# A gated linear attention with a gated scan behind it: second group's attention ahead of the first projection, and an input weight that comes in two halves

## The chip, the cores and the metric

One core of one Trainium2 chip runs the whole kernel. The metric is the device time of one execution in microseconds (us). TensorE (PE) does matmuls and transposes, VectorE (DVE) scans and element-wise work, ScalarE (ACT) activations and copies, GpSimd (POOL) element-wise work, SyncE (SP) only hands out transfers. ACT and POOL can hand out transfers too.

## The reference

Two blocks, joined by a change of layout. All data are float32 but for the weights of the second block: these arrive as 64-bit floats (8 bytes an element), and the kernel makes 32-bit floats of them itself.

```python
# q, k, v, alpha: (B=4, H=8, S=768, D=48)
for t in range(S):
    state = alpha[:, :, t, :, None] * state + einsum('bhd,bhe->bhde', k[:, :, t], v[:, :, t])
    y[:, :, t] = einsum('bhd,bhde->bhe', q[:, :, t], state)
x = y.transpose(0, 2, 1, 3).reshape(B, S, 384)

proj = x @ w_in                      # w_in: (384, 1024)
val, gate = proj[..., :512], proj[..., 512:]
h = 0
for t in range(S):
    h = exp(A_log) * h + val[:, t]
    ys[:, t] = h
out = (silu(gate) * ys) @ w_out      # w_out: (512, 384)
```

## The kernel before, in words

The work is cut into N = 12 groups of GC = 256 positions, three for each batch entry, in order; a group has two chunks (c = 0, 1) of 128. Each group goes through two parts.

**Attention of a group.** Its alpha, k and q are loaded (`load_natural` L420 for the first three groups, `load_raw` L405 after these), v too (`load_v` L429). The first three groups are turned on PE (`natural_alpha` L556, `natural_qk` L567), the later ones on DVE (L590). `products` makes running products of alpha with a scan on DVE (prod, L599) and their inverses with a second (inv, L611). k times inv and q times prod make the tile Z (L573; `k_times`, `q_times`). Then `scores` (PE, L645), `keys` (PE transposes of Z, L635, copied by ACT to ktm, L636), `masks` (A: half by DVE from PSUM, L653, half copied by ACT, L651, and multiplied by POOL, L652), `values` (PE, L664), `state` (PE, L685, copied by ACT to S_sb, L688, for the next chunk; the next `state` adds to the same PSUM tile st, so it follows that copy), `carried` (PE, L675). `join` copies the result to xT (ACT, L694 and L695) and moves pieces of it between partitions with six small transfers (L698), handed out by POOL for groups 0 and 1, by SP and ACT for later ones.

**Projection of a group.** `project(n, cc)` for cc = 0 to 3 multiplies xT with columns cc of w_in (pv and pg, L713); `gated` scans pv on DVE (hh, L720), takes silu of pg on ACT (sg, L725) and multiplies both on POOL (f, L726). `output` multiplies f with w_out (L734), ACT copies (L738), SP stores (L739).

**Weights.** The bits of w_in lie over 128 partitions in bits_in: heads 0 to 3 (192 rows of w_in) on partitions 0 to 63, heads 4 to 7 on partitions 64 to 127. Four transfers bring them (L443): partitions 0-47, 64-111, 48-63, 112-127. The bits of w_out come in two (L448). `convert(i)` makes float32 of one quarter of the columns of w_in (i < NI = 4) or one half of w_out (i = 4, 5): ACT prepares wr from the low words (L510), DVE shifts and joins the high words (L511, L513), POOL adds both (L515). wr has two buffers. A float32 column quarter is needed by `project(n, cc)` of the same number.

**Order.** It is written out by hand: each engine takes its instructions in the order of the program text, and so do the queues of transfers of SP and ACT. Eight completion semaphores are shared by the transfers of SP and ACT in turn, so a transfer also waits for the one eight before it. The text has a prologue (loads of groups 0 and 1 and of the weights, attention of group 0, products of group 1, `warm`, which runs five matmuls that nobody reads), and then the loop over n = 0 to 11, in which iteration n projects group n, does attention of group n + 1, products of group n + 2, and loads group n + 3. Iterations 0 and 1 differ from the others: in iteration 0 the conversions stand between the projections, in iteration 1 Z of group 2 is made. The buffers of alpha, k and q are two per name (group modulo 2), those of v too; Z, hh, sg and the rest have two; PSUM has three tiles "mm" for pv, pg, output and transposes.

At the end a flag tells whether the running products stayed in range; a second, general function would run if not. It does not run with these inputs.

Of the kernel before, what the change touches and what calls it, by code (L numbers as in the profile page):

```python
# [346 lines left out]
def fast(  # L347
# [18 lines left out]
    nc = tc.nc  # L366
    B, H, S, D = q.shape
# [3 lines left out]
    G = 2  # L371
    GC = G * C
    NG = S // GC
    N = B * NG
    NT = GC // 32
    NK = DM // C
    NI = DI // C
    R = D - 32
# [47 lines left out]
    def load_v(m, engine, cs=range(G)):  # L426
        b, g = divmod(m, NG)
        for c in cs:
            engine.dma_start(out=vs[m % NV][:, c, :, 0:D],  # L429
                             in_=v[b, :, ds(g * GC + c * C, C), :].rearrange("h p d -> p h d"))  # L430
# [6 lines left out]
    bits_in = const.tile([C, NK, 2 * DI, 2], U32, name="bits_in")  # L437
    bits_out = const.tile([C, NI, DM, 2], U32, name="bits_out")

    def load_w_in(engine):  # L440

        for row, size, first, step in ((0, D, 0, D), (64, D, 4 * D, D), (D, R, 3 * D, R), (64 + D, R, 7 * D, R)):
            engine.dma_start(out=bits_in[ds(row, size)].rearrange("p kk n two -> p kk (n two)"),  # L443
                             in_=moe_w_in.bitcast(U32)[ds(first, NK * step)]
                             .rearrange("(kk p) n -> p kk n", p=step)[0:size])
# [51 lines left out]
    def convert(i):  # L497


        if i < NI:  # L500
            bits = bits_in.rearrange("p kk (vg n) two -> p kk vg n two", vg=2)[:, :, :, ds(i * C, C)]
            w = w_in[:, :, :, ds(i * C, C)]
        else:
            rows = ds(2 * (i - NI), 2)
            bits, w = bits_out[:, rows, None], w_out[:, rows, None, :]
        lo, hi = bits[..., 0], bits[..., 1]
        _, x, y, z = w.shape
        r = p2.tile([C, x, y, z], I32, tag="wr", name="wr")
        t = w.bitcast(U32)
        nc.scalar.activation(r, lo, AF.Copy, scale=2.0 ** -29)  # L510
        nc.vector.tensor_scalar(out=t, in0=hi, scalar1=3, scalar2=0x3FFFFFFF,  # L511
                                op0=ALU.logical_shift_left, op1=ALU.bitwise_and)
        nc.vector.scalar_tensor_tensor(out=t, in0=hi, scalar=0xC0000000, in1=t,  # L513
                                       op0=ALU.bitwise_and, op1=ALU.bitwise_or)
        return lambda: nc.gpsimd.tensor_tensor(out=w.bitcast(I32), in0=w.bitcast(I32), in1=r, op=ALU.add)  # L515
# [43 lines left out]
    def natural_qk(m, name):  # L559

        if m not in Zs:
            Zs[m] = p2.tile([C, 4, 2, GC], FP32, tag="Z", name="Z")
        tps = []
        for c in range(G):
            tp = ps_sc.tile([C, 4, C], FP32, tag=f"sc{c}", name="tn")
            for p in range(4):
                nc.tensor.transpose(tp[:, p, :], natural(name, m)[:, c, 2 * p:2 * p + 2, :], ident)  # L567
            tps.append(tp)

        def times(c):  # L570
            i, by = {"k": (1, invs), "q": (0, prods)}[name]
            cols = ds(c * C, C)
            nc.vector.tensor_mul(Zs[m][:, :, i, cols], tps[c], by[:, :, cols])  # L573
        return times
# [73 lines left out]
    def masks(m, c):  # L648
        A, sc = As[m, c]
        mb = mask[:, None, :].to_broadcast([C, 4, C])  # L650
        nc.scalar.activation(A[:, 1], sc[1], AF.Copy)  # L651
        nc.gpsimd.tensor_mul(A[:, 1], A[:, 1], mb)  # L652
        nc.vector.tensor_mul(A[:, 0], sc[0], mb)  # L653
# [94 lines left out]
    def pair(name, m, one, other):  # L748
        load_natural(name, m, 0, one)
        load_natural(name, m, 1, other)  # L750
# [5 lines left out]
    pair("q", 0, SP, SP)  # L756
    pair("a", 1, SP, SP)
    load_v(0, SP)
    load_w_in(SP)
    pair("k", 1, SP, SP)  # L760
    pair("q", 1, SP, SP)
    for i in range(2):
        load_w_out(i, SP)
    load_v(1, SP)

    constants()

# [9 lines left out]
    for name in "akq":  # L777
        pair(name, 2, SP, SP)

    def warm():  # L780

        t = ps_mm.tile([C, 4, C], FP32, tag="mm", name="warm")
        for _ in range(5):
            nc.tensor.matmul(t, ident, ident[:, None, :].to_broadcast([C, 4, C]), start=True, stop=True)

    warm()
    for _ in products(0):
        pass
    for c in range(G):
# [3 lines left out]
        scores(0, c)  # L793
    for c in range(G):
        masks(0, c)
    for c in range(G):
        keys(0, c)
    natural_alpha(1)
# [7 lines left out]
    state(0, 1)  # L806
    carried(0, 1)
    join(0, (nc.gpsimd, nc.gpsimd))
    convert(0)()
    warm()  # L810
    k_times, q_times = natural_qk(1, "k"), natural_qk(1, "q")
    for _ in steps:
        pass
    for c in range(G):
        k_times(c)
        q_times(c)

    checks = itertools.chain.from_iterable(check_w(i) for i in range(NW))
    value = None
    for n in range(N):  # L820
        m = n + 1
        att = m < N
        nat = n + 2 < NAT
        steps = products(n + 2) if n + 2 < N else iter(())

        def go(count):
            for _ in range(count):
                next(steps, None)


        if n + 3 < N:
            loads(n + 3)
        if n + 2 < N:
            load_v(n + 2, SP)

        def attend():
            for c in range(G):
                keys(m, c)
            for c in range(G):
                scores(m, c)  # L840


        pj = project(n, 0)
        gated(n, 0, *pj)
        if n == 0:
            convert(1)()
        if n == 1:
            for c in range(G):
                k_times(c)
                q_times(c)  # L850
        elif att:
            attend()
        if not nat:
            go(1)
        if n == 1:
            pj = project(n, 1)
            gated(n, 1, *pj)
            attend()
        if att:
            for c in range(G):  # L860
                masks(m, c)
        if n == 0:
            convert(2)()
        if n != 1:
            pj = project(n, 1)
            gated(n, 1, *pj)
        if n == 0:
            convert(3)()
        if not nat:
            go(1)  # L870
        pj = project(n, 2)
        gated(n, 2, *pj)
        if n == 0:
            convert(4)()
            convert(5)()
        if not nat:
            go(2)
        if att:
            state(m, 0)
            values(m, 0)  # L880
            values(m, 1)
            state(m, 1)
            carried(m, 0)
            carried(m, 1)
            join(m, (nc.gpsimd, nc.gpsimd) if n == 0 else (SP, ACT))
        pj = project(n, 3)
        gated(n, 3, *pj)
        if nat:
            natural_alpha(n + 2)
            check_alpha(n + 2)  # L890
        go(10)
        if 3 <= n:
            for _ in itertools.islice(checks, 2):
                pass
        if n == N - 2:
            check_end()
        if n == N - 1:
            value = nc.values_load(flag[0:1, 0:1], min_val=0, max_val=1)
        output(n)
        if nat:  # L900
            k_times, q_times = natural_qk(n + 2, "k"), natural_qk(n + 2, "q")
    return value


# [36 lines left out]
```

## Time and profile before

| | |
|---|---|
| median of 9 runs | 329.07 us (328.16 to 331.33) |
| the profiled execution, its own time | 326.13 us |
| its span in the profile | 324.3 us |
| PE busy | 292.2 us (90%), 2351 matmuls |
| DVE busy | 229.4 us (71%) |
| ACT, POOL busy | 97.1 us (30%), 113.6 us (35%) |
| read from memory, written | 33.33 MB, 4.72 MB |
| iterations 3 to 10 together (start of the first pv, 124.69 to 302.92) | 178.2 us |

The span is from the first to the last instruction of the profiled execution; its own time holds what lies around it, and the median is over runs without a profile. Starts are counted from the begin of the span. A row of the page or of a trace answer gives the line of the kernel, the engine, the operation, what it writes and reads, how many, and durations; "idle before" is the time in which the engine had nothing to run, with the instruction or transfer that ended it. PEclk is the share of TensorE's full clock that was granted.

### The profile page before, as it was taken

The numbers are of one execution on the slowest core, as the hardware profiler recorded it, in microseconds if no ns is written. First come the engines' busy times: TensorE is split into PE (matmuls) and PEld (weight loads), VectorE is DVE, ScalarE is ACT, GpSimd is POOL, SyncE is SP. The second block draws the span as 40 slices with busy tenths as digits, with TensorE's granted clock in tenths as the row PEclk, the third lists the DMA queues.
The fourth block names the chain that finished last, engine by engine and source line by source line (L and its number), as shares of the span: only waits on it lengthen the run. The fifth ranks groups of instructions, "written<-read, shape, count | busy, mean of one in ns | idle before, by whom it ended". The sixth has DMA issues, their size and how long they took to land.

```text
span 324.3 us, 5980 instructions
## 1 busy us (share of the span) xinstructions
PE 292.2 (90%) x2351; PEld 232.0 (72%) x2351; DVE 229.4 (71%) x244; ACT 97.1 (30%) x200; POOL 113.6 (35%) x109
## 2 busy tenths in 40 slices
PE   2994195999995999999999999999999999999992
PEld 2681074868764887878868878878688688786771
DVE  3850298967991896898998998989979689432110
ACT  4160115433220434225214224242253142231111
POOL 6033028770710610722704216408134054150020
PEclk9999569999997999999999999999999999999998
DMA  9999999958159915925919629559288130100101
GB/s 132 170 144 135 133 280 173 233 74 215 23 115 204 207 17 141 218 34 155 219 39 238 125 81 232 85 136 219 39 212 168 50 61 6 57 1 14 49 5 56
DMA packets 66029, 39.71 MB, mean 122 GB/s; under 512 B 47044, under 2 KB 65096, under 8 KB 65608
## 3 DMA queue, kind: packets, MB, share of 16 engines
q1 hardware_dynamic: 63600, 38.35, 60.3%
q10 hardware_dynamic: 2008, 0.69, 1.1%
q8 instruction: 20, 0.33, 0.5%
q0 software_dynamic: 384, 0.20, 0.4%
q14 instruction: 17, 0.14, 0.2%
HBM read 33.33 MB, written 4.72 MB: 117 GB/s over the span
## 4 chain that ended last, share of the span: by engine, by line
PE 73%; DMA 10%; DVE 7%; SPq 4%; POOL 3%; issue 1%; ACT 0%; POOLq 0%; DVEq 0%
PE pv L713 19%; PE o L734 18%; PE pg L713 16%; DMA raw_k<-in_k_dram 8%; PE sc L645 6%; PE y L664 5%; PE y L675 3%; PE st L685 3%; SPq L420 2%; PE tp L635 2%; POOL A L652 1%; PE tn L567 1%; DVE w_out L513 1%; DVE w_in L513 1%; DVE w_in L511 1%; DMA raw_a<-in_alpha_dram 1%
## 5 line engine op out<-in xcount | busy, mean ns | idle before, releaser
L726 POOL TENSOR_TENSOR f<-sg,hh 128x256 f32<-128x256 f32 x48 | 59.4, 1237 | 152.6 <-ACT sg L725 143.0
L713 PE MATMUL pv<-xT,w_in 128*128 128x256 f32 x288 | 74.6, 396 | 6.9 <-DMA xT<-xT 3.5
L713 PE MATMUL pg<-xT,w_in 128*128 128x256 f32 x288 | 70.1, 379 | 0.0
L713 PEld LDWEIGHTS pv<-xT,w_in 128*128 128x128 f32 x288 | 54.1, 195 | 19.7 <-issue 6.2
L734 PE MATMUL o<-w_out,f 128*128 128x384 f32 x192 | 64.3, 487 | 0.5 <-POOL f L726 0.5
L713 PEld LDWEIGHTS pg<-xT,w_in 128*128 128x128 f32 x288 | 55.0, 191 | 7.5
L734 PEld LDWEIGHTS o<-w_out,f 128*128 128x128 f32 x192 | 36.3, 190 | 23.6 <-POOL f L726 1.1
L725 ACT ACTIVATE sg<-pg 128x256 f32<-128x256 f32 x48 | 18.4, 383 | 115.7 <-PE pg L713 98.7
L720 DVE TENSOR_TENSOR_SCAN hh<-a_dec,hh,pv 128x256 f32<-128x256 f32 x32 | 23.4, 732 | 38.5 <-PE pv L713 36.5
L652 POOL TENSOR_TENSOR A<-A,mask 128x512 f32<-128x512 f32 x24 | 32.3, 1366 | 27.4 <-ACT A L651 27.4
L599 DVE TENSOR_TENSOR_SCAN prod<-aT,first 128x1024 f32<-128x1024 f32 x12 | 33.1, 2762 | 0.1
L611 DVE TENSOR_TENSOR_SCAN inv<-aT,last 128x1025 f32<-128x1025 f32 x12 | 31.0, 2585 | 0.4
L738 ACT ACTIVATE o_sb<-o 128x384 f32<-128x384 f32 x24 | 11.8, 490 | 48.3 <-PE o L734 48.3
L645 PE MATMUL sc<-Z 48*128 48x128 f32 x384 | 25.1, 279 | 0.0
L645 PEld LDWEIGHTS sc<-Z 48*128 48x128 f32 x384 | 22.7, 188 | 2.8 <-issue 2.0
L664 PE MATMUL y<-A,v 128*64 128x128 f32 x384 | 23.6, 274 | 0.5 <-POOL A L652 0.5
L653 DVE TENSOR_TENSOR A<-sc,mask 128x512 f32<-128x512 f32 x24 | 16.5, 690 | 7.5 <-PE sc L645 7.2
L664 PEld LDWEIGHTS y<-A,v 128*64 128x64 f32 x384 | 20.7, 137 | 0.9 <-POOL A L652 0.7
L590 DVE STREAM_TRANSPOSE aT<-raw_a 128x1024 f32<-128x1024 f32 x9 | 18.4, 2040 | 0.0
L590 DVE STREAM_TRANSPOSE Z<-raw_q 128x1024 f32<-128x1024 f32 x9 | 18.3, 2031 | 0.0
L590 DVE STREAM_TRANSPOSE Z<-raw_k 128x1024 f32<-128x1024 f32 x9 | 18.2, 2021 | 0.0
L720 DVE TENSOR_TENSOR_SCAN hh<-a_dec,pv 128x256 f32<-128x256 f32 x16 | 10.9, 679 | 9.1 <-PE pv L713 9.1
(86 smaller groups left out, 268.4 us busy)
## 6 DMA issues: line engine op xcount, KB each, us to landing
raw_k<-in_k_dram SPq DMA_DIRECT2D x24, 192.0 KB, 5.2
raw_q<-in_q_dram SPq DMA_DIRECT2D x24, 192.0 KB, 5.5
v<-in_v_dram SPq DMA_DIRECT2D x24, 192.0 KB, 4.4
out_dram<-o_sb SPq DMA_DIRECT2D x24, 192.0 KB, 1.9
raw_a<-in_alpha_dram SPq DMA_DIRECT2D x23, 192.0 KB, 3.9
raw_a<-in_alpha_dram SPq DMA_DIRECT2D x18, 176.0 KB, 4.2
raw_k<-in_k_dram SPq DMA_DIRECT2D x18, 176.0 KB, 5.1
raw_q<-in_q_dram SPq DMA_DIRECT2D x18, 176.0 KB, 4.8
```

The costliest lines, as they stand in the source:

```text
L590: nc.vector.transpose(out=to.rearrange("p h (c j) -> p h j c", j=NT), in_=raw_bufs[m % NR][name].rearrange("p h (j d) -> p h j d", d=D)[:, ...
L599: nc.vector.tensor_tensor_scan(out=prod, data0=aT[:, 0:4 * GC], data1=first.rearrange("p h n -> p (h n)"), initial=0.0, op0=ALU.mult, op1= ...
L611: nc.vector.tensor_tensor_scan(out=inv[:, ::-1], data0=aT[:, ::-1], data1=last.rearrange("p h n -> p (h n)")[:, 0:4 * GC + 1][:, ::-1], in ...
L645: nc.tensor.matmul(sc[i][:, p, :], Z[rows, p, 1, cols], Z[rows, p, 0, cols], start=True, stop=True)
L652: nc.gpsimd.tensor_mul(A[:, 1], A[:, 1], mb)
L653: nc.vector.tensor_mul(A[:, 0], sc[0], mb)
L664: nc.tensor.matmul(ys[m][i][ds(64 * s, 64), e, ds(c * C, C)], v_sb[:, c, 2 * p + i, :], A[:, i, p, :], start=(c == 0 and e == 0), stop=Fal ...
L713: nc.tensor.matmul(pj, w_in[:, kk, vg, ds(cc * C, C)], xT[:, kk, :], start=(kk == 0), stop=(kk == NK - 1))
L720: nc.vector.tensor_tensor_scan(out=hh, data0=a_dec[:, cc:cc + 1].to_broadcast([C, GC]), data1=pv, initial=prev_h[cc][:, GC - 1:GC] if g el ...
L725: nc.scalar.activation(sg, pg, AF.Silu)
L726: nc.gpsimd.tensor_mul(fs[n][:, cc, :], sg, hh)
L734: nc.tensor.matmul(os[c], fs[n][:, cc, ds(c * C, C)], w_out[:, cc, :], start=(cc == 0), stop=(cc == NI - 1))
```

## The change

Four things are done, all in the prologue and in iterations 0 and 1. `load_w_in` takes a half and an engine: half 0 (partitions 0-63) is handed out by SP, after k and q of group 1, half 1 (partitions 64-127) by ACT, after the mask copies of group 0; v of group 1 goes ahead of w_out. The attention of group 1 (scores, keys, masks, state, values, carried, join) stands ahead of the loop, and iteration 0 has none. The four conversions of w_in stand between the masks and the state of group 1; those of w_out stand in iteration 0. Alpha of group 2 is turned in iteration 0 between projections 1 and 2, and Z of group 2 is made at the end of iteration 0. `warm` before group 1's scores runs four matmuls, not five, and stands after the transposes of k and q.

```diff
-    def load_w_in(engine):
-        for row, size, first, step in ((0, D, 0, D), (64, D, 4 * D, D), (D, R, 3 * D, R), (64 + D, R, 7 * D, R)):
+    def load_w_in(half, engine):
+        for row, size, first, step in ((64 * half, D, 4 * half * D, D), (64 * half + D, R, (4 * half + 3) * D, R)):
...
     load_v(0, SP)
-    load_w_in(SP)
     pair("k", 1, SP, SP)
     pair("q", 1, SP, SP)
+    load_w_in(0, SP)
+    load_v(1, SP)
     for i in range(2):
         load_w_out(i, SP)
-    load_v(1, SP)
...
     for c in range(G):
         masks(0, c)
+    load_w_in(1, ACT)
     for c in range(G):
         keys(0, c)
...
     join(0, (nc.gpsimd, nc.gpsimd))
-    convert(0)()
-    warm()
     k_times, q_times = natural_qk(1, "k"), natural_qk(1, "q")
+    warm(4)
     for _ in steps:
         pass
     for c in range(G):
         k_times(c)
         q_times(c)
 
+    for c in range(G):
+        scores(1, c)
+    for c in range(G):
+        keys(1, c)
+    for c in range(G):
+        masks(1, c)
+    for i in range(NI):
+        convert(i)()
+    state(1, 0)
+    values(1, 0)
+    values(1, 1)
+    state(1, 1)
+    carried(1, 0)
+    carried(1, 1)
+    join(1, (nc.gpsimd, nc.gpsimd))
...
-        att = m < N
+        att = 0 < n < N - 1
...
         gated(n, 0, *pj)
-        if n == 0:
-            convert(1)()
-        if n == 1:
-            for c in range(G):
-                k_times(c)
-                q_times(c)
-        elif att:
+        if att:
             attend()
...
-        if n == 1:
-            pj = project(n, 1)
-            gated(n, 1, *pj)
-            attend()
         if att:
             for c in range(G):
                 masks(m, c)
-        if n == 0:
-            convert(2)()
-        if n != 1:
-            pj = project(n, 1)
-            gated(n, 1, *pj)
-        if n == 0:
-            convert(3)()
-        if not nat:
+        pj = project(n, 1)
+        gated(n, 1, *pj)
+        if nat:
+            natural_alpha(n + 2)
+            check_alpha(n + 2)
+            convert(NI)()
+        else:
             go(1)
         pj = project(n, 2)
         gated(n, 2, *pj)
-        if n == 0:
-            convert(4)()
-            convert(5)()
-        if not nat:
+        if nat:
+            convert(NI + 1)()
+        else:
             go(2)
...
-            join(m, (nc.gpsimd, nc.gpsimd) if n == 0 else (SP, ACT))
+            join(m, (SP, ACT))
         pj = project(n, 3)
         gated(n, 3, *pj)
-        if nat:
-            natural_alpha(n + 2)
-            check_alpha(n + 2)
         go(10)
...
         if nat:
             k_times, q_times = natural_qk(n + 2, "k"), natural_qk(n + 2, "q")
+            for c in range(G):
+                k_times(c)
+                q_times(c)
```

`nat` holds in iteration 0 alone (n + 2 < 3); `go` takes that many steps of the products of group n + 2.

More of the change, by code (lines that the diff above doesn't have):

```diff
@@ L778, in fast, with warm @@
         pair(name, 2, SP, SP)
-    def warm():
+    def warm(count):
         t = ps_mm.tile([C, 4, C], FP32, tag="mm", name="warm")
-        for _ in range(5):
+        for _ in range(count):
             nc.tensor.matmul(t, ident, ident[:, None, :].to_broadcast([C, 4, C]), start=True, stop=True)
-    warm()
+    warm(5)
     for _ in products(0):
@@ L808, in fast @@
     join(0, (nc.gpsimd, nc.gpsimd))
-    convert(0)()
-    warm()
     k_times, q_times = natural_qk(1, "k"), natural_qk(1, "q")
+    warm(4)
     for _ in steps:
```

## The prediction

> **What bounds the kernel now.** I read the page first (spans, the 40 slices), then the chain of waits in order of time, then the waits, then stretches of the first 60 us, then the timeline. From the page, the PE row, the granted clock and the DMA rate in 40 slices of 8.1 us:
>
> ```profile
> PE   2994195999995999999999999999999999999992
> PEclk9999569999997999999999999999999999999998
> GB/s 132 170 144 135 133 280 173 233 74 215 23 115 204 207 17 141 218 34 155 219 39 238 125 81 232 85 136 219 39 212 168 50 61 6 57 1 14 49 5 56
> ```
>
> From the fourteenth slice on PE is full, so only the first 105 us can give anything back. Two holes show: slices 4 and 5, and slice 13. The chain of waits names what ends them (start, us, what):
>
> ```profile
> 13.99 27.18 DMA raw_k<-in_k_dram
> ...
> 44.36 2.01 PE pv L713 x6
> ...
> 55.31 1.78 DVE w_in L511
> 57.11 1.36 DVE w_in L513
> ...
> 98.36 2.48 DMA xT<-xT
> 100.89 2.90 PE pv L713 x6
> ...
> 124.69 1.30 PE pv L713 x6
> ```
>
> Iteration 0 starts at 44, but crawls behind DVE's conversion of w_in; iteration 1 ends in a wait for the xT moves; iteration 2 starts at 100.89 and iteration 3 at 124.69. From there to the start of iteration 11 (302.92) eight iterations take (302.92 - 124.69)/8 = 22.3 us each, PE alone. The waits from 24 to 104 us (us in total, times, longest) confirm that the first hole is data:
>
> ```profile
> DVE w_in L511 <- DMA bits_in<-in_moe_w_in_dram: 14.7, 1, 14.7
> PE tn L567 <- DMA raw_k<-in_k_dram: 12.0, 2, 11.6
> PE pv L713 <- DMA xT<-xT: 3.5, 1, 3.5
> ```
>
> Stretches (last columns: granted clock, DMA share, GB/s):
>
> ```profile
> 4.00:13.00 9.00, 7.28 (x29) 6.13 (x30) 4.19 (x8) 3.66 (x7) 1.95 (x5) 1.00 1.53 163
> 15.00:22.00 7.00, 6.97 (x92) 5.77 (x92) 3.85 (x8) 4.29 (x9) 2.52 (x2) 1.00 1.00 131
> 22.00:23.00 1.00, 1.00 (x30) 0.94 (x30) 1.00 (x1) 0.20 (x1) 0.00 (x0) 1.00 0.80 164
> 43.00:46.00 3.00, 3.00 (x13) 2.59 (x12) 2.90 (x4) 0.00 (x0) 0.00 (x0) 0.55 1.03 404
> ```
>
> The 3.15 MB of w_in move at 131 GB/s, while w_out, which follows over all 128 partitions, moves at 404. The first w_in transfer writes partitions 0-47, the second 64-111, then 48-63, 112-127, one after another on SP. In the packets, an 8 KB packet of w_in takes 0.95 to 1.1 us while one side is written, and 0.51 to 0.54 us around 22.7, where half the engines have gone on to the other side: 16 x 8 KB / 0.52 us = 250 GB/s. And group 1's k and q queue behind all of it:
>
> ```profile
> 13.52 11.88 SPq L420 DMA_DIRECT2D raw_k<-in_k_dram  x2
> 25.44 14.07 SPq L420 DMA_DIRECT2D raw_q<-in_q_dram  x2
> ```
>
> SP is held in these issues: the load behind can't be handed over while w_in fills the queue.
>
> **What the Trainium skill says.** "SBUF — State Buffer", Door 1: The DMA port swizzle: 64 partitions reach only 8 of 16 ports (196 GB/s measured there). The trace agrees in kind, at 131. Same page, "Can I just issue two DMAs to hit both halves?": no, two concurrent ones brought 6%. The trace's 22.7 us speaks against that, but has no second queue in it. "DMA: Bandwidth & Descriptors", Issuing engines are not separate DMA queues: they interleave on the same engines. The trace agrees: from 2.6 to 3.4 us packets of ACT's and SP's loads alternate about 1:1. "TensorE: Matmul & The Clock Gate", Part 1: after some 3.4 us without work the clock halves. Agrees: PE idle from 28.1, clock 0.5 from 32.0, PE back at 39.7, full again at 45.7.
>
> **The change, part by part.**
>
> 1. SP's order. k1 and q1 take w_in's place. A natural load holds SP 1.14 us, so q1's second is handed over near 15.4 and lands 3.5 to 4 us later (the loads of a1 do): 19, not 43.1. The first half of w_in starts near 17.7 (its first packet now 13.1, plus four loads of 1.15).
> 2. ACT issues the second half after its mask copies (these end at 18.87): two issues of 0.43 to 0.6, so 1 us on ACT. Queued behind them: ktm, aT, the alpha check of group 1; so the products on DVE and the S_sb and xT copies come 1 us later. If both halves write at once at 250 GB/s, w_in is there at 17.7 + 2.5 (alone, 0.33 MB) + 2.82/0.25 = 31.5, with landing about **33**. That is my choice; the other end is 131 throughout, 24 us from 17.7 and v1 and w_out between: 44.
> 3. Group 1's attention ahead of the loop. PE carries group 0 to 24.6 (23.56 + 1), transposes k1, q1 (2.0) to 26.6, warm 4 x 0.94 to 30.4; DVE's scan of products ends 24.7, the next 27.5, four Z of 0.68 to 30.2. Scores 30.4 to 32.5, keys to 33.4, ktm on ACT to 34.1, A copies to 35.3, POOL's masks 2 x 1.26 to **37.2**.
> 4. All of w_in converted at once, on POOL behind these masks: 4 x 1.81 from C = max(37.2, w_in + 1.6) (DVE's 0.56 + 0.96 first). ACT's third and fourth wr wait for a buffer, so for POOL's first and second add; S_sb stands behind them on ACT: C + 3.65 + 0.9 + 0.4. PE's second state matmuls wait for that S_sb; with carried (0.6 + 1.1) the projection starts at **C + 6.7 = 43.9**, just when it does now (43.94), yet with attention 1 done and w_in converted. POOL's xT moves (2.9 us) follow at C + 8; xT of group 1 is wanted 19 us later. The f of iteration 0 queue behind them to about C + 19.3; output wants the last at P0 + 15.5 = C + 22.2: hidden, with 3 us of cover.
> 5. Iteration 0 loses attention (PE 1.04 + 2.06 + 1.34 + 1.93 + 1.09 = 7.5 us, moved into the wait for w_in) and the conversion stalls. Left on PE: four projections 10.5, alpha 1.0, output 5.3, transposes 2.1 = 18.9. The w_out conversions and products of group 2 stand beside it (DVE 3.8 + 2.4 + 5.5 in 19 us): nothing, while w_out and a2 are there. a2's issue waits for w_in's transfers, then lands within 9 us: 42, wanted at 49.
> 6. Iteration 1 becomes an ordinary one, 22.3. q_times of group 2 end 2.7 us into it: keys wait 0.6. The 3.5 us wait for xT goes: SP's q loads of group 4 stood until 92.4, when ACT's xT moves completed; with the transfers renumbered nothing holds SP there. What is late next is DVE, 19 us of work in 22.
>
> Sum, with P0 the start of projection 0: after = P0 + 18.9 + 22.3 + (324.3 - 100.9) - 1.4 (iteration 2's first pv 2.90 at half clock, else 1.49) + x = P0 + 263.2 + x. x is what the page doesn't show: PE idles most of 33.4 to 42 and then runs some 5 us at half clock, 2.5; the keys 0.6; early DVE/POOL collisions, unknown, 0 to 3, taken 1.5. **43.9 + 263.2 + 4.6 = 311.7**, that is 12.6 under the profiled span of 324.3. That execution's own time is 326.13, under the median of 329.07; taken off the median: 316.5. Own range 313 to 320.
>
> **The rivals.**
>
> - The halves don't overlap (the change doesn't do what its second queue says). For: the skill's 6%; POOL's xT moves, issued at 25, began only at 34.4 when the w_in packets ended, so a queue can be starved. Against: the alternation at 2.6 us. Then w_in 44, P0 = 44 + 1.6 + 6.7 = 52.3, x 3.1: span 318.6, time 323.4.
> - Slower: ACT is held at its issue of the second half. SP sat 11.4 us in one k1 issue because the queue behind was full of w_in; here v1's second load stands behind the first half the same way, from about 18.8, and ACT comes at 18.9. If both issue through one generator that stalls in order, ACT is held until the half and v1's first load have drained, 32.3. For: at the start the ACT and SP issues stretch one another (a_log's 0.82 against 0.43). Against: they also alternate, so may be kept apart. Price: ktm 33.4, aT 34.7, scans to 40.1, PE at half clock, scores at 45.5, POOL masks done 52.5, P0 = 59.2; x 3.4: 325.8, time 330.6. It decides from a hold that ends after some 31 us; under that the sum is below 324.3.
>
> **The numbers.** Overlap 0.43 (316.5), no overlap 0.25 (323.4), ACT held 0.32 (330.6, of that 0.2 slower, 0.06 within, 0.06 faster). Within 0.3% (1 us, about what can be told here from no change) counts as the same. So faster 0.74, same 0.06, slower 0.20. The range reaches from the lower end of the first case to the centre of the third: 313 to 330.5.
>
> **What would show it.** Right: raw_k of group 1 landed by 19; w_in stretch near 250 GB/s; ACT's L443 issues under 0.7 us each; POOL's first w_in add at 37; first pv at 44, first pv of iteration 2 near 89 and no xT wait before it; 22.3 per iteration after. Wrong: an ACT issue of over 5 us (third case); 131 GB/s until 40 (second); a wait of PE in iteration 0 for POOL's f or in iteration 1 for DVE's Z of over 2 us.

## The result, and the profile after

The changed kernel takes **325.21 us** (median of 10 runs, 322.16 to 328.21) against 329.0 us for the kernel before (31 runs beside it): ratio 0.9853, 95% interval 0.9819 to 0.9888. The ratios, here and in the table below, leave out executions more than 1.5% above the fastest of their kernel (three of the ten here); for e3 this left too few for a ratio, and the traces of e3 and e5 are of such executions, so that no totals are read from these two. So the changed kernel is faster by 3.8 us in the medians, 4.8 by the ratio, and not by the 12.5 us of the forecast. The profiled execution of after has a span of 323.7 us and a time of its own of 325.41 us, near its median. That of before (span 324.3, own time 326.13) was 2.9 us faster than its median, so the two traces differ by 0.6 us in span where the medians differ by 3.8. Stretches are therefore compared one by one, and totals by the medians.

From the page of after, PE's busy share, its granted clock and the DMA rate in 40 slices:

```profile
PE   2998156969999999999999999999999999999991
PEclk9999657977999999999999999999999999999999
GB/s 132 163 161 156 133 259 174 230 71 93 228 65 124 229 47 177 201 15 223 156 68 228 105 114 231 53 173 203 17 202 179 74 35 12 52 1 14 49 5 56
```

Slice 13, the second hole of before, is full now. The first hole is still there (slices 5 to 7), and the ninth slice (65 to 73 us) has a new one; the slices at 5 to 7 tenths of the clock are in these holes and behind them. The chain of waits of after (start, us, what) names them:

```profile
18.69 24.33 DMA bits_in<-in_moe_w_in_dram
...
43.17 1.74 ACT wr L510 x2
44.91 1.99 POOL w_in L515
...
46.93 0.94 ACT wr L510
47.87 1.99 POOL w_in L515
...
50.78 0.22 ACT S_sb L688
...
52.92 2.86 PE pv L713 x6
...
66.45 3.75 POOL w_out L515
...
70.25 7.12 PE o L734 x12
...
100.84 1.29 PE pv L713 x6
```

Half 1 of w_in, handed out by ACT at 18.69, is on the chain for 24.33 us. Then come the conversions, with S_sb of group 1 behind them on ACT, then a projection at half clock (2.86 us for six matmuls, 1.29 later), then POOL's conversion of w_out and an output at half clock (7.12 us for 12 matmuls). Iteration 2 starts near 100.8, and no xT wait stands before it. The waits from 24 to 104 us (us in total, times, longest) add what PE waited for:

```profile
DVE w_in L511 <- DMA bits_in<-in_moe_w_in_dram: 10.8, 1, 10.8
...
PE st L685 <- DMA v<-in_v_dram: 9.8, 1, 9.8
...
PE o L734 <- POOL w_out L515: 2.9, 1, 2.9
```

Stretches of after (stretch, length, busy time of PE, PEld, DVE, ACT, POOL; granted clock, DMA share, GB/s):

```profile
19.00:26.00 7.00, 6.70 (x107) 5.82 (x106) 4.38 (x6) 4.72 (x10) 2.31 (x3) 1.00 1.04 143
28.00:31.00 3.00, 3.00 (x28) 1.81 (x28) 1.54 (x4) 0.00 (x0) 0.43 (x1) 1.00 0.98 178
32.00:39.00 7.00, 1.40 (x10) 1.04 (x9) 0.42 (x1) 2.06 (x4) 2.48 (x2) 0.74 1.05 144
52.00:56.00 4.00, 4.00 (x36) 3.08 (x29) 1.80 (x2) 1.42 (x3) 3.04 (x3) 0.57 1.07 191
```

143 GB/s while half 0 comes, 144 while half 1 comes; 178 only in between, where both sides are written. The timeline shows how the transfers were handed out:

```profile
17.38 1.59 SPq L429 DMA_DIRECT2D v<-in_v_dram  x2
18.32 0.82 ACTq L443 DMA_DIRECT2D bits_in<-in_moe_w_in_dram  x2
19.02 19.58 SPq L448 DMA_DIRECT2D bits_out<-in_moe_w_out_dram  x1
```

ACT was not held (0.82 us for two). SP was: 19.58 us in the first issue of w_out.

Start of the first pv matmul of the first four iterations in each trace, and the times. The ratio is to runs of before on the same chip; e13 had a single run.

| kernel | it. 0 | it. 1 | it. 2 | it. 3 | median us | ratio, interval |
|---|---|---|---|---|---|---|
| before | 44.15 | 74.78 | 100.89 | 124.53 | 329.0 | |
| after | 52.85 | 78.95 | 100.68 | 122.85 | 325.21 | 0.9853 [0.9819, 0.9888] |
| e1 both halves on SP | 54.96 | 77.86 | 103.11 | 128.12 | 328.45 | 0.9983 [0.9953, 1.0013] |
| e2 v handed out early | 53.81 | 80.08 | 101.80 | 123.97 | 324.82 | 0.9864 [0.9785, 0.9943] |
| e3 state ahead of conversions | 52.85 | 79.13 | 100.85 | 123.03 | 324.76 | |
| e4 w_out converted earlier | 53.59 | 75.42 | 97.14 | 119.31 | 321.03 | 0.9767 [0.9690, 0.9844] |
| e5 halves in pieces | 62.44 | 88.77 | 110.50 | 132.67 | 333.49 | 1.0121 [1.0089, 1.0153] |
| e6 halves in turn on SP | 49.60 | 74.35 | 99.60 | 123.53 | 326.11 | 0.9848 [0.9742, 0.9954] |
| e7 before, k and q first | 48.79 | 82.87 | 108.58 | 133.77 | 334.65 | 1.0162 [1.0096, 1.0227] |
| e8 attention's end in iteration 0 | 47.86 | 73.00 | 94.73 | 116.90 | 318.95 | 0.9680 [0.9616, 0.9744] |
| e9 as e6, small ones from ACT | 47.83 | 69.48 | 91.21 | 113.38 | 317.52 | 0.9673 [0.9616, 0.9730] |
| e10 e8 and e9 together | 42.50 | 67.73 | 89.45 | 111.63 | 313.67 | 0.9545 [0.9499, 0.9591] |
| e11 before, other semaphore | 43.26 | 73.33 | 95.72 | 117.89 | 322.02 | 0.9804 [0.9763, 0.9846] |
| e12 packets of 4 KB | 52.16 | 78.36 | 100.09 | 122.26 | 323.42 | 0.9832 [0.9767, 0.9897] |
| e13 xT moves later | 54.09 | 80.30 | 102.02 | 124.19 | 326.51 | |
| e14 no adds on w_in | 49.76 | 74.47 | 96.20 | 118.37 | 318.62 | 0.9687 [0.9538, 0.9836] |

### The profile page after: what moved, and what is told of

Same layout as the page of the kernel before. It is cut to its first block, busy times and chain, and to the rows that moved or that the text cites. A ratio compares the mean times of both kernels' runs of the same rounds, so it can differ in the third digit from the quotient of the medians.

```text
span 323.7 us, 5980 instructions
## 1 busy us (share of the span) xinstructions
PE 293.7 (91%) x2349; PEld 233.6 (72%) x2349; DVE 227.1 (70%) x244; ACT 97.0 (30%) x200; POOL 115.5 (36%) x109
## 4 chain that ended last, share of the span: by engine, by line
PE 84%; DMA 9%; POOL 3%; ACT 1%; DVE 1%; issue 0%; ACTq 0%; POOLq 0%
PE pv L713 21%; PE o L734 20%; PE pg L713 18%; DMA bits_in<-in_moe_w_in_dram 8%; PE sc L645 7%; PE y L664 5%; PE y L675 3%; PE st L685 3%; PE tp L635 2%; PE tn L567 2%; PE warm L784 1%; DMA a_log<-in_moe_A_log_dram 1%; POOL w_in L515 1%; POOL w_out L515 1%; ACT wr L510 1%; PE tn L556 1%
## 5 line engine op out<-in xcount | busy, mean ns | idle before, releaser
L726 POOL TENSOR_TENSOR f<-sg,hh 128x256 f32<-128x256 f32 x48 | 60.5, 1260 | 144.4 <-ACT sg L725 142.5
L713 PE MATMUL pv<-xT,w_in 128*128 128x256 f32 x288 | 73.6, 392 | 0.0
L734 PE MATMUL o<-w_out,f 128*128 128x384 f32 x192 | 67.4, 506 | 2.9 <-POOL w_out L515 2.9
L734 PEld LDWEIGHTS o<-w_out,f 128*128 128x128 f32 x192 | 37.7, 198 | 27.9 <-POOL w_out L515 3.9
L720 DVE TENSOR_TENSOR_SCAN hh<-a_dec,hh,pv 128x256 f32<-128x256 f32 x32 | 23.5, 734 | 33.5 <-PE pv L713 31.5
L652 POOL TENSOR_TENSOR A<-A,mask 128x512 f32<-128x512 f32 x24 | 29.9, 1269 | 35.5 <-ACT A L651 35.5
L611 DVE TENSOR_TENSOR_SCAN inv<-aT,last 128x1025 f32<-128x1025 f32 x12 | 29.4, 2451 | 0.4
L664 PE MATMUL y<-A,v 128*64 128x128 f32 x384 | 25.2, 286 | 0.0
L685 PE MATMUL st<-v,ktm 128*64 128x48 f32 x320 | 13.5, 228 | 12.4 <-DMA v<-in_v_dram 9.8
L685 PEld LDWEIGHTS st<-v,ktm 128*64 128x64 f32 x320 | 11.8, 142 | 16.3 <-issue 13.0
L664 PEld LDWEIGHTS y<-A,v 128*64 128x64 f32 x384 | 22.4, 145 | 0.2 <-issue 0.2
L590 DVE STREAM_TRANSPOSE aT<-raw_a 128x1024 f32<-128x1024 f32 x9 | 18.3, 2038 | 0.0
```

Of the source, the lines that this page charges most:

```text
L590: nc.vector.transpose(out=to.rearrange("p h (c j) -> p h j c", j=NT), in_=raw_bufs[m % NR][name].rearrange("p h (j d) -> p h j d", d=D)[:, ...
L611: nc.vector.tensor_tensor_scan(out=inv[:, ::-1], data0=aT[:, ::-1], data1=last.rearrange("p h n -> p (h n)")[:, 0:4 * GC + 1][:, ::-1], in ...
L664: nc.tensor.matmul(ys[m][i][ds(64 * s, 64), e, ds(c * C, C)], v_sb[:, c, 2 * p + i, :], A[:, i, p, :], start=(c == 0 and e == 0), stop=Fal ...
L685: nc.tensor.matmul(st[ds(64 * i, 64), p, :], ktms[c][:, p, i, :], vs[m % NV][:, c, 2 * p + i, 0:D], start=(ch == 0 and p == 0), stop=(ch = ...
L713: nc.tensor.matmul(pj, w_in[:, kk, vg, ds(cc * C, C)], xT[:, kk, :], start=(kk == 0), stop=(kk == NK - 1))
L720: nc.vector.tensor_tensor_scan(out=hh, data0=a_dec[:, cc:cc + 1].to_broadcast([C, GC]), data1=pv, initial=prev_h[cc][:, GC - 1:GC] if g el ...
```

## The experiments

### Where the gain came from: e1, e7, e11

**e1.** Both halves on SP, one behind the other; all else as changed.

```diff
-    load_w_in(0, SP)
+    for i in range(2):
+        load_w_in(i, SP)
     load_v(1, SP)
...
-    load_w_in(1, ACT)
```

> Both halves of w_in on SP, half 1 right behind half 0, ahead of v of group 1; ACT hands out none of it. Theory A (one generator makes the packets of both queues in order; SP's load of v stood ahead of half 1 in it, so half 1 ran behind half 0 anyway): nothing to lose, w_in there at 42 to 43.5 as in the changed kernel (43.1), v of group 1 after it at 44 to 45, span within 1.5 us of 323.7. Rival (the second queue did bring overlap, some 3 us of it): w_in there at 46, span 3 us longer.

328.45 us, no difference from before that can be told. The last packet of w_in starts at 42.3 instead of 40.9: the second queue saves 1.4 us. But iterations 1 and 2 take 25.2 and 25.0 us (21.7 and 22.2 in after). The timeline of e1 shows why:

```profile
79.25 3.18 SPq L405 DMA_DIRECT2D raw_k<-in_k_dram  x4
...
93.01 1.86 ACTq L698 DMA_DIRECT2D xT<-xT  x3
...
94.87 1.86 SPq L405 DMA_DIRECT2D raw_q<-in_q_dram  x4
```

SP stops behind raw_k and hands out raw_q of group 4 the moment ACT's xT moves of group 2 are through, just as in before. SP's own xT moves stand behind that, and PE waits 3.4 us for them at 103. In the traces of before and e1 this load has the same one of the eight completion semaphores as ACT's first xT move, and it is handed out when that move has landed (move landed at 92.39 and load handed out at 92.47 before, 94.80 and 94.87 in e1); in after the two have different ones. All sixteen traces agree: in the four in which SP hands out all of w_in (before, e1, e6, e7) the load has the move's semaphore and is held, and in the twelve in which ACT hands out a part of it, it has another and is not held by the move.

**e7.** The kernel before, with k and q of group 1 ahead of w_in, and nothing else.

```diff
-    load_w_in(SP)
     pair("k", 1, SP, SP)
     pair("q", 1, SP, SP)
+    load_w_in(SP)
```

> The kernel before with one edit: k and q of group 1 loaded ahead of w_in, all of w_in on SP. This prices the loads' new place alone: w_in, and with it the first projection, 4 to 5 us later (first pv 48.5 to 49.5 instead of 44.2), nothing else moved. If the time before iteration 2 is bound by w_in, 332 to 334; if by the late k and q of group 1 (their transposes and products in iteration 1), most of that comes back and it is 328 to 330.

334.65 us, 6.2 more than before beside it. The first pv came at 48.79, as expected, and w_in's delay was then paid in full and more: the first two iterations took 34.1 and 25.7 us (30.6 and 26.1). The loads' new place is a cost; the changed kernel has to earn it back with group 1's attention.

**e11.** The kernel before, with w_in's two small transfers (partitions 48-63 and 112-127) handed out by ACT behind its mask copies; the two large ones (0-47, 64-111) stay on SP. It serves to shift the count of semaphores and little else.

```diff
-    load_w_in(SP)
+    load_w_in(SP, slice(0, 2))
...
         masks(0, c)
+    load_w_in(ACT, slice(2, 4))
```

> The kernel before with one edit: the two small 16-row transfers of w_in are issued by ACT behind its mask copies, the large ones stay on SP. w_in may land up to 2 us later; what matters is the count of semaphores: raw_q of group 4 no longer waits for ACT's xT move. Theory: this wait (3.5 us of PE before iteration 2, then 1.4 us at half clock) is worth 3 to 5 us alone, so 324 to 326, as fast as the whole change. Rival: the gain of the changed kernel comes from group 1's attention and w_in, and the wait is covered by something else: 328 to 330.

322.02 us. The ACT transfers run beside the end of SP's, so that w_in is also there 1.2 us sooner (wr 37.25, before 38.45). In the timeline of e11, raw_q is no longer held:

```profile
74.72 1.79 SPq L405 DMA_DIRECT2D raw_k<-in_k_dram  x4
...
76.62 4.65 SPq L405 DMA_DIRECT2D raw_q<-in_q_dram  x4
...
89.14 1.87 ACTq L698 DMA_DIRECT2D xT<-xT  x3
```

Iteration 1 takes 22.4 us instead of 26.1, iteration 2 22.2 instead of 23.6. Two issues in another queue bring 6.6 us, more than the whole change. With the wait put back, in e1, the change is worth nothing that can be told (e1 also gives up the second queue, and with it the 1.4 us in w_in), and the loss of the wait alone, in e11, is worth more than the change, also if the 0.9 us by which e11's first pv is ahead are taken off. The table says the same: at the first pv of iteration 1 the changed kernel is 4.2 us behind before (78.95 against 74.78), and it makes up 5.9 us in iterations 1 and 2, where the wait was.

### Why the halves did not overlap: e2, e5, e12, e13, e6, e9

**e2.** v of group 1 handed out by ACT at about 10 us, so that SP's queue holds only half 0.

```diff
     load_w_in(0, SP)
-    load_v(1, SP)
...
     check_alpha(0)
+    load_v(1, ACT)
```

> v of group 1 is handed out by ACT at about 10 us, ahead of everything of w_in, so that no load with many packets stands between the two halves. Theory A (the generator was held by v): first packet of half 1 at 20 to 21 instead of 27, both halves alternate, over 200 GB/s, w_in there at 34 to 36, first pv near 46, time 5 to 7 us under the changed kernel. Theory B (an engine serves a whole transfer of one queue before it turns to the other): half 1 begins at 27 to 28 again, w_in there at 42 to 44, first pv at 52 to 53, time as the changed kernel.

324.82 us, as after. Here ACT's half came first (first packet 20.44) and SP's stood still until 26.90. From the DMA view of e2, queues from 20 to 26.5 us (packets, MB, share of 16 engines; q10 is ACT's, q1 SP's):

```profile
q10 hardware_dynamic: 110, 0.90, 97.4%
q1 hardware_dynamic: 737, 0.14, 20.5%
```

SP's 737 packets are small ones, 0.14 MB in all. The queues have changed places, so v's load was not what held the second; whichever is first runs alone for a while, 6.5 us here and 9.1 in after. Also, v of group 1 had landed by 17.41 instead of 43.77 and 44.99, and the first pv came no sooner (53.81): the 9.8 us for which PE waited for v in after were not what set the first projection.

**e5.** Each half in pieces: three packets per DMA engine in a transfer, not nine.

```diff
-            engine.dma_start(out=bits_in[ds(row, size)].rearrange("p kk n two -> p kk (n two)"),
-                             in_=moe_w_in.bitcast(U32)[ds(first, NK * step)]
-                             .rearrange("(kk p) n -> p kk n", p=step)[0:size])
+            for kk in range(NK):
+                engine.dma_start(out=bits_in[ds(row, size), kk].rearrange("p n two -> p (n two)"),
+                                 in_=moe_w_in.bitcast(U32)[ds(first + kk * step, size)])
```

> The changed kernel with each half of w_in in pieces by chunk (three transfers of 48 rows, three of 16; three packets of 8 KB per DMA engine instead of nine), SP with half 0 and ACT with half 1 as before. Theory B (a DMA engine serves a whole transfer of one queue before it turns to the other): turns now come every three packets, the engines drift apart and both sides are written for a good part; w_in's last packet near 36 us instead of 40.9, wr near 38 to 39, first pv near 47 to 49, time 319 to 322. Rival C (the first queue runs until it is empty whatever the size of its transfers): half 1 begins again only near 27, last packet at 41, first pv at 53, time 325.

333.49 us. ACT's first packet at 25.96, the last at 40.94: Theory B falls. And ACT was now held, as in the third case of the prediction. Timeline of e5:

```profile
18.33 15.16 ACTq L444 DMA_DIRECT2D bits_in<-in_moe_w_in_dram  x6
...
50.24 3.53 POOL L652 TENSOR_TENSOR A<-A,mask 128x512 f32<-128x512 f32 x2 [5.46 <-ACT A L651]
```

Six issues took ACT from 18.33 to 33.49. What stood behind them (aT, ktm, A copies) came late, POOL's masks at 50.24 instead of 35.35, first pv at 62.44. The mechanism is real; the changed kernel's two issues did not set it off.

**e12.** Packets of 4 KB: the 48-row transfers cut in two along the row.

```diff
+            for s in range(2 if size == D else 1):
+                cut = ds(s * 2 * DI, 2 * DI) if size == D else ds(0, 4 * DI)
+                engine.dma_start(out=bits_in[ds(row, size)].rearrange("p kk n two -> p kk (n two)")[:, :, cut],
+                                 in_=moe_w_in.bitcast(U32)[ds(first, NK * step)]
+                                 .rearrange("(kk p) n -> p kk n", p=step)[0:size, :, cut])
```

> The changed kernel with the 48-row transfers of both halves cut in two along the row: packets of 4 KB instead of 8 (the 16-row transfers stay). In all runs so far the second queue's first packet came after 7 to 10 packets of 8 KB per engine of the first queue, counted from its issue. Theory D (an engine has a fixed number of packets of the first queue taken ahead): ACT's first packet now after 9 to 10 packets of 4 KB, near 22 to 23.5 us instead of 27.3; both sides are written from then on, w_in's last packet near 37 to 39, first pv 49 to 51, time 320 to 323. Rival T (a fixed number of bytes or a time of 8 us, or the end of SP's first large transfers): ACT's first packet at 26 to 27 again, last packet at 41, first pv 53, time 325.

323.42 us. ACT's first packet came at 26.74, after 19 packets of 4 KB per engine, where after had ten of 8 KB: not a number of packets, so Theory D falls. Its rival named three things: an amount of data, a time, or the end of SP's first large transfer. e11 speaks against the last: there ACT's first packet came at 27.20, 9.0 us after its issue, though SP's w_in had been running since 13.20 and its first large transfer had landed at 23.85.

**e13.** POOL's xT moves of group 0 later, at 37 us.

```diff
+        if m:
+            moves(m, engines)
+
+    def moves(m, engines):
+        xT = xTs[m]
         for s in range(2):
...
         masks(1, c)
+    moves(0, (nc.gpsimd, nc.gpsimd))
```

> The changed kernel with POOL's six xT moves of group 0 issued behind its masks of group 1 (near 37 us) instead of at 25 us; nothing else moved. If these moves are what lets the second queue start, or what holds it, ACT's first packet of w_in moves away from 27.3 by several us (before 22 or after 34). If it is what SP's queue had already handed to the DMA engines, ACT's first packet stays between 26 and 28 us and the time at 325, with xT of group 0 landing by 44, long before its use at 53.

ACT's first packet at 27.07: the moves have nothing to do with it. What is left is an amount of data, 71 to 83 KB per DMA engine moved since the issue of the second queue's transfer, or a time, 7.2 to 9.1 us since that issue, over all runs with two queues. At the rates of these runs the two are the same, and which it is stays open.

**e6.** All of w_in on SP, in the pieces of e5, half 0 and half 1 in turn.

```diff
...
+        for kk in range(NK):
+            for half in range(2):
+                row, first = 64 * half, (4 * half + kk) * D
+                engine.dma_start(out=bits_in[ds(row, D), kk].rearrange("p n two -> p (n two)"),
+                                 in_=moe_w_in.bitcast(U32)[ds(first, D)])
...
-    load_w_in(1, ACT)
```

> The changed kernel with all of w_in on SP in one queue, in the same pieces by chunk, half 0 and half 1 in turn. If the rate is set by the side that is written (131 GB/s for one, up to 250 for both), engines that run ahead reach the other side's piece and the rate rises over 131: w_in's last packet between 32 and 38 us, first pv 44 to 50, time 317 to 323. If the engines stay in step, or the rate belongs to the size of packets and not to the side, it stays at 131: last packet at 42, first pv at 55, as with both halves on SP in a row (328.4).

w_in's last packet at 37.6, wr at 40.03 instead of 43.17, first pv at 49.60. The stretches of e6 that answer to those of after:

```profile
19.00:26.00 7.00, 6.79 (x108) 6.03 (x107) 4.68 (x6) 4.60 (x10) 2.59 (x4) 1.00 1.00 183
28.00:31.00 3.00, 3.00 (x34) 2.00 (x34) 1.54 (x3) 0.00 (x0) 0.15 (x1) 1.00 1.02 178
```

183 GB/s, from one queue, where after has 143 from 19 to 26 us; the same pieces without the turns, in e5, gave 149. So it is not a second queue or the size of the pieces that raises the rate here, but the turns between the halves. The two halves differ in the partitions that are written and also in the rows of memory that are read; no run separates these, so that it is the side written is the likely reading and is not shown. The time was 326.11 all the same, above the 317 to 323 expected: SP's raw_q of group 4 was held until 91.38 here, for ACT's xT moves again.

**e9.** e6 with the small transfers (16 rows) handed out by ACT, which shifts the count of semaphores as in after.

```diff
-    load_w_in(1, ACT)
+    for half in range(2):
+        ACT.dma_start(out=bits_in[ds(64 * half + D, R)].rearrange("p kk n two -> p kk (n two)"),
+                      in_=moe_w_in.bitcast(U32)[ds((4 * half + 3) * D, NK * R)]
+                      .rearrange("(kk p) n -> p kk n", p=R))
```

> The kernel of e6 (w_in's six large pieces on SP, half 0 and half 1 in turn) with the two small 16-row transfers of w_in issued by ACT where the changed kernel has its second half. That moves the count of the transfers' semaphores, so that SP's raw_q load of group 4 no longer waits for the semaphore that ACT's xT move holds. If that wait is what e6 lost again, SP issues raw_q of group 4 at once (near 78, not 91), there is no xT wait before iteration 2 and the time is 321 to 323 against 326.1 for e6. If the wait has another cause, 326.

317.52 us; raw_q at 72.77, no wait before iteration 2. That is more than expected: w_in is another 1.1 us sooner (last packet at 36.48), and the clock is full again at 44.9, before the first pv, and stays so. In the stretches shown for e6 the rates are 173 and 180 GB/s here.

### The conversions and iteration 0: e3, e14, e4

**e3.** state, values and carried of group 1 ahead of the conversions.

```diff
+    state(1, 0)
+    values(1, 0)
+    values(1, 1)
+    state(1, 1)
+    carried(1, 0)
+    carried(1, 1)
     for i in range(NI):
         convert(i)()
-    state(1, 0)
...
-    carried(1, 1)
```

> State, values and carried of group 1 stand ahead of the conversions of w_in in the order of all engines. Theory (S_sb stood behind wr on ACT, and wr behind POOL's adds): S_sb is copied at about 44.6, the first pv moves from 52.9 to 47 to 49, and the time goes down by 3 to 4 us. Rival (POOL's chain of adds, xT moves, f and w_out adds sets the end of iteration 0 and doesn't move): the first pv moves but the first pv of iteration 1 (78.95) moves by under 1.5 us.

324.76 us (319.12 to 325.64), not to be told from after: a miss. The wait changed its owner: wr now stood behind the second S_sb on ACT, at 50.04 instead of 43.17. Timeline of e3:

```profile
49.81 0.33 ACT L688 ACTIVATE S_sb<-st 128x192 f32<-128x192 f32 x1 [4.22 <-PE y L675]
50.04 1.66 ACT L510 ACTIVATE wr<-bits_in 128x768 int32<-128x768 uint32 x2
51.00 7.09 POOL L515 TENSOR_TENSOR w_in<-w_in,wr 128x768 int32<-128x768 int32 x4 [12.78 <-ACT wr L510]
```

It shows one thing by the way: with DVE long done, POOL's four adds follow one another in 7.09 us, 1.77 each.

**e14.** POOL's adds on w_in left out.

```diff
     for i in range(NI):
-        convert(i)()
+        convert(i)
```

> The changed kernel without POOL's four adds on w_in (the low bits of w_in are left out of the weights); ACT's wr and DVE's two instructions of each conversion stay. If POOL's add and DVE's L513 take turns (1.99 + 0.96 = 2.95 us per conversion), L513 takes 0.96 us in all four, the four conversions take 4 x 1.55 = 6.2 us from 43.2, S_sb of chunk 0 comes near 47 instead of 50.7 and the first pv at 49 to 50 instead of 52.9: the time falls by 3 to 4 us. If L513 is slow for another reason (the w_out load filling SBUF, ACT's reads of the same tile), it stays near 2.44 us and first pv near 52.

318.62 us, 6.6 under after where 3 to 4 were expected. DVE's second step of the conversion in after and in e14 (min/median/max in ns, first and last start):

```profile
L513 DVE SCALAR_TENSOR_TENSOR w_in<-bits_in,w_in x4: 958/2443/2461, 43.8 to 51.2; 128x768 uint32<-128x768 uint32 x4
```

```profile
L513 DVE SCALAR_TENSOR_TENSOR w_in<-bits_in,w_in x4: 959/959/962, 44.1 to 48.5; 128x768 uint32<-128x768 uint32 x4
```

L513 takes 0.96 us alone and 2.44 beside POOL's add. One conversion in after takes 2.95 us, which is 1.99 (add) plus 0.96: the two take turns, and 1.81 was the add alone. The Trainium skill names this contention ("SBUF — State Buffer", Who interferes with whom: a DVE instruction with two SBUF inputs contends with a GpSimd instruction that reads SBUF); this trace agrees, and adds the price. The first pv came 3.1 us earlier, as expected, and iteration 0 is 1.4 us shorter, its first projection being at full clock; the span is 4.9 us shorter. The rest of the 6.6 is within the spread of the two runs that e14 had (316.73 and 320.51).

**e4.** Both w_out conversions right behind projection 0 of iteration 0.

```diff
     gated(n, 0, *pj)
+    if n == 0:
+        convert(NI)()
+        convert(NI + 1)()
...
     check_alpha(n + 2)
-    convert(NI)()
```

> Both conversions of w_out stand right behind projection 0 of iteration 0, not behind projections 1 and 2 and the turn of alpha. Theory (output waited for POOL's second w_out add, 2.9 us, and ran at half clock after that wait, 3.2 us): the wait goes, the clock stays, first pv of iteration 1 at 73 to 74 instead of 78.95, time 4 to 6 us less. Rival (the half clock comes anyway from the idle time before): 3 us less. Second rival: POOL's f of projections 1 to 3 come later by the adds and hold output as long: under 1 us.

321.03 us. In after, wr of w_out stood behind aT and the alpha check on ACT (62.27), POOL's two adds ended at 65.77 and 70.19, the second taking 3.78 us beside DVE's scan of 2.64 us, and f of the last projection stood behind them. In e4 the adds end at 64.14, and the chain of e4 has a whole output at full clock, 16 matmuls in 5.16 us, where after waited 2.86 us and then took 7.12 for the last 12:

```profile
67.38 1.29 PE pg L713 x6
68.67 5.16 PE o L734 x16
73.83 1.75 PE tn L567 x16
```

Iteration 0 takes 21.8 us instead of 26.1. Iteration 1 began at 75.42, later than the 73 to 74 expected.

The wait and the half clock behind it are not one thing. The same wait, 2.86 or 2.87 us at the same place, stands in ten of the traces. In e1 and e9 the 12 matmuls behind it then took 4.14 us, at full clock; in e6 5.54, in e3 5.83, in the other six 7.12 to 7.21. What decides between these is not shown.

### Versions that beat both: e8, e10

**e8.** e4, and the end of group 1's attention (state, values, carried, join) behind projection 0 of iteration 0. The first pv then needs only the first conversion.

```diff
-    state(1, 0)
...
-    join(1, (nc.gpsimd, nc.gpsimd))
...
     gated(n, 0, *pj)
+    if n == 0:
+        state(1, 0)
+        values(1, 0)
+        values(1, 1)
+        state(1, 1)
+        carried(1, 0)
+        carried(1, 1)
+        join(1, (nc.gpsimd, nc.gpsimd))
+        convert(NI)()
+        convert(NI + 1)()
```

> The kernel of e4 (w_out converted behind projection 0 of iteration 0) with the last part of group 1's attention (state, values, carried, join) moved behind the same projection, ahead of the w_out conversions. The first pv then needs only the first conversion: 47 us instead of 53.6. If PE's order was what held the projection, iteration 1 begins 2 to 4 us sooner than in e4 (75.4): 71.5 to 73.5, time 317 to 319. If the conversions at 2.95 us each hold the projection all the same, or S_sb waits behind the sg copies, iteration 1 begins at 75 and the time is 321.

318.95 us, as the first case said (first pv 47.86, iteration 1 at 73.00).

**e10.** e8 with the loads of e9.

> e8 (last part of group 1's attention and the w_out conversions behind projection 0) with w_in loaded as in e9. If the parts add up: w_in there near 40 instead of 44, first pv near 43 to 44, iteration 1 near 70, time 315 to 317 (e8: 319). If group 1's attention, or the crawl of the projection behind the conversions (2.95 us each), sets iteration 1 instead of w_in, 318 to 319.

**313.67 us**, 0.9545 of before, the fastest of all and under the 315 to 317 expected. Most of the two gains adds up: it is 11.5 us under after, where e8 is 6.3 and e9 7.7 under it. Its chain:

```profile
38.73 1.71 ACT wr L511 x2
...
40.46 2.00 POOL w_in L516
...
42.50 2.93 PE pv L714 x6
45.43 2.56 PE pg L714 x6
47.99 0.92 PE st L686 x16
...
60.99 5.16 PE o L735 x16
66.15 1.75 PE tn L568 x16
```

From 42.50 on PE has no wait of more than 0.5 us. What is left is the half clock of the first 12 matmuls (2.93 and 2.56 us, 1.29 later) and w_in itself.

## Why the prediction was right and wrong

The sign, the range (313 to 330.5) and the wait that goes were right; the size was not, and 325.21 lies outside the 313 to 320 of the case that was chosen. The prediction's sum for the span, P0 + 18.9 + 22.3 + 222.0 + x with P0 = 43.9 and x = 4.6, gave 311.7. The trace of after gives 52.85 + 26.1 + 21.7 + 223.0 = 323.7. The 12.0 us between them lie here:

- **P0: +8.95, of that +7.7 by step 2, the step that failed.** Step 2 chose the overlap of the halves at 250 GB/s, with w_in there at 33. It landed at 43.0 (143 and 144 GB/s, 178 for 4 us). What failed first was the overlap itself: 10 of half 0's 12 packets per engine had started before half 1's first. The evidence I had set against the skill's 6%, packets of two queues that alternate from 2.6 to 3.4 us, was of 192-byte packets; 8 KB packets alternate too, but only after the time in which the first queue runs alone (9.1 us in after). By e1 the second queue is worth 24.1 to 22.7 us from the first packet to the last start, 6%, near the +6% over a single transfer that the Trainium skill states ("SBUF — State Buffer", "Can I just issue two DMAs to hit both halves?"); it says that the two serialize, which these runs confirm for the beginning.
- **The rate in step 2** failed too. The 250 GB/s multiplied the time of eight packets near 22.7 us by 16 engines, in a stretch that the prediction's own line shows at 164 GB/s with a DMA share of 0.80. Where both sides were written the rate was 178 in after and 199 in e2 (28 to 35 us); with 180 in place of 250, step 2 gives 35.9 instead of 31.5 (an estimate), and e9, which writes both sides in turn, started its last packet at 36.48.
- **P0 by step 4: +1.2.** Its order of waits held, with C at 44.9 (7.7 late, all of it w_in); P0 = C + 6.7 was C + 7.9. The pace of 1.81 was mis-sized, 2.95 (e14); x held 1.5 for collisions of DVE and POOL, called unknown there.
- **Iteration 0: +7.2.** Step 5 cost the conversions of w_out at nothing, "while w_out and a2 are there". They were there; what failed was that ACT and POOL came to them late. In after this is 2.9 us of wait and 3.0 us of half clock in the output (7.12 us where e9 has 4.14 for the same matmuls); e4, which converts earlier, has neither. Another 1.6 is the half clock of the first pv and pg (2.86 and 1.38 against 2.6 for both), which the sum had in x. The three make 7.5; the rest of the iteration was 0.3 under its 18.9.
- **x: -4.6**, since what came of it is counted above. **Iteration 1: -0.6**, 21.7 against 22.3. **From iteration 2 on: +1.0.**

The no-overlap rival, given 0.25, said w_in 44 and P0 52.3, both within 1 us. That its time, 323.4, comes within 1.8 us is luck: its span, 318.6, is 5.1 too short, and the trace of before, from which it counts, is 2.9 us under its median.

Right were step 1 (q1 landed at 20.2, forecast 19, not 43.1; half 0's first packet at 18.18, forecast 17.7), step 3 (POOL's masks done at 37.8, forecast 37.2), and step 6 in what it priced. The wait for xT was put there at 3.8 us in iteration 1 and 1.4 in iteration 2 by the sum; e11 has 3.7 and 1.5. That it would go was in part luck: the step says that the transfers are renumbered, not which semaphore the load gets, and in e1 and e6, also renumbered, it got the move's again. This wait is what the change earns; the other 7.4 of the 12.6 us in the forecast were to come from w_in and group 1's attention, and these bring nothing as they stand (4.2 us behind at iteration 1, and e1). The third case did not occur (ACT's issues 0.33 and 0.44 us), but e5 shows its mechanism, with the price near the one given (333.49; given 330.6).

## What to carry to other kernels

When a transfer is moved between queues, look at which completion semaphore the later transfers get and who else holds it: two issues moved from SP to ACT were worth more here than the whole rearrangement, and a gain of this kind says nothing about the change that brought it. Two transfers that fill the lower and the upper 64 partitions did better here cut and put in turn into one queue than in two queues, of which the second started late. A rate worked out from a few packets is to be compared with what the same stretch moved. And where a step is costed at nothing because it lies beside other work, follow it on every engine through which it passes. Idle time of PE can bring half clock behind it, but not at a fixed price: the same wait of 2.9 us cost between nothing and 3.1 us more.

## What the hardware showed that I had not expected

- The queue that comes second started 7.2 to 9.1 us after its issue when the first had large transfers waiting, whether these were of 9 or 3 packets per engine, of 8 or 4 KB (27.29, 25.96 and 26.74 us in after, e5 and e12, with issues at 18.3).
- Small packets suffer longest beside large ones: in after, from 31 to 40 us v's 192-byte packets went out one for one with half 1's 8 KB packets, some 16 of these per us, so v of group 1, issued at 17.4, landed only at 43.8 and 45.0.
- An engine that hands out a transfer can be held by it for a long time: SP 19.58 us in after, ACT 15.16 us for six in e5.
- The order of the pieces sets the rate: 143 to 149 GB/s while only one half was loaded (after, e5), 183 and 178 with the halves in turns of 48 rows, from one queue (e6).
